# Retention and token-mixing MLP in one kernel: nine of the loads of k issued by ScalarE on its own DMA queue

## The chip, the cores and the metric

The kernel runs on one core of one Trainium2 chip. The metric is the device time of one execution in microseconds; below the time is better. One execution was profiled, and three others were timed without a profile.

The core has five engines that follow their own instruction lists in order: TensorE (PE, with its weight loads shown apart as PEld), VectorE (DVE), ScalarE (ACT), GpSimd (POOL) and SyncE (SP). A transfer is issued by an instruction in the list of one of them and then carried out by the core's 16 DMA engines. In the views, ACTq and SPq stand for ScalarE and SyncE while they issue a transfer.

## What is computed

The reference, cut to what matters (B 4, H 8, S 768, D 64, model width 512):

```python
gamma = 1.0 - 2.0 ** (-5.0 - np.arange(H))
for t in range(S):
    state = gamma * state + einsum('bhd,bhe->bhde', k[:, :, t], v[:, :, t])
    y[:, :, t] = einsum('bhd,bhde->bhe', q[:, :, t], state) / sqrt(D)
x = y.transpose(0, 2, 1, 3).reshape(B, S, H * D)

wq, wk = x @ w_q, x @ w_k
W_tok = einsum('bsd,btd->bst', wq, wk) / sqrt(64)
mixed = einsum('bst,btd->bsd', W_tok, x)
out = maximum(mixed, 0.0) @ w_out
```

A recurrence over the tokens gives x; a mixing of all tokens of a batch, a ReLU and a projection follow. All inputs and the output are float32: q, k and v are 6.29 MB each, the weights 1.31 MB and the output 6.29 MB.

## The kernel before

**The work.** The tokens are cut into 12 pairs of chunks, of 256 tokens each, three pairs to a batch. A pair is the unit of all that follows. Its k and q are loaded as float32, cast to bfloat16 and transposed; its v is loaded and scaled by a power of the decay. TensorE then forms the scores, the state and the rows of x, and in a later stage the mixing and the projection. Small steps do this, and each is one function:

- `ck`, `cq`: cast of k and of q (lines 623, 641, 660, through the helper `copy`, lines 138 to 141); `cv`: scaling of v on GpSimd (line 650). In pairs 2 to 11 `ck` and `cv` come in two parts, 0 and 1, each of two instructions on 64 partitions.
- `trk`, `trq`: transposes on TensorE (lines 667 and 700); `ek`, `eq`: their copies out of PSUM to `kq` (lines 689 and 725).
- `sc`, `eat`: scores and their masked copy (lines 740 and 757); `st`, `es`: state and its copy (lines 799 and 823); `in`, `ia`: the two parts of y (lines 779 and 828); `ex`: y to x (line 845).
- `xt`, `exT`, `wk`, `wq`, `ew`: x transposed and its products with the two small weights; `zm`, `ez`: their product with x per batch and its copy to `z_sb` (lines 948 and 966).
- `mx`, `r`, `pj`, `eo`: mixing, ReLU, projection and the copy of half an output to `o_st` (lines 976, 992, 1001 and 1013).

**The order of the work.** It is written out by hand. `ORDER` (line 16) is a list of tokens such as `cq.5:A`: step `cq` of pair 5 on ScalarE (A; V is VectorE, P is GpSimd); `@b` gives a PSUM bank. The loop at line 1050 emits them one by one, so each engine's list is the list of its tokens in this order. No scheduler changes it.

**The loads.** `LOADS` (line 55) is a second list: `k5` is the load of k of pair 5, `w`, `o0` and `o1` are weights, `s1` the store of output 1. `more_loads` (line 243) emits the loads in this order on SyncE, as far as the staging slots go (`SLOTS` is 7; a slot holds one input of three pairs and comes free when all three were cast). It is called when a slot comes free (`release`, line 261) and after each `eo`. So SyncE's list holds all loads in the order of `LOADS` and then the stores; the only transfer on another engine is half of the first k (line 240, ScalarE). A load of k or v of a pair is one transfer of 512 KB in rows of 512 bytes; a load of q is two transfers of 256 KB in rows of 1 KB (lines 170 to 176; in pairs 0 and 1 it is one transfer). Line 171 is the issue of q, line 188 that of k and v, line 223 that of `o0` and `o1`, line 1035 that of the stores.

**Completion semaphores.** In the built program all transfers, whichever engine issues them, take eight completion semaphores in turn. Before a transfer is issued, its issuing engine waits until the transfer eight places earlier, which had the same semaphore, has landed. So no more than eight transfers are under way.

Of the kernel before, what the change touches and what calls it, by code (L numbers as in the profile page):

```python
# [13 lines left out]


ORDER = """
ck.0.0:V ck.0.1:V fill.13@6 cv.0.1:P cq.0.0:A trk.0@0 fill.2@6 cq.0.1:V trq.0@0 ekq.0.1:V fill.2@6 fill.2@6
cv.0.0:P fill.2@6 fill.2@6 ekq.0.0:V sc.0.1@2 eat.0.1:V sc.0.0@0 st.0.0 fill.2@6 fill.2@6 ck.1:A trk.1@4
cq.1:A ck.2.1:A es.0.0:V in.0@2 eat.0.0:V ck.2.0:A ic.0@2 trq.1@4 ekq.1.1:V ekq.1.0:V cv.1:P ia.0.1@2
ia.0.0@2 st.0.1 es.0.1:V ex.0:V cv.3.0:P fill.2@6 cv.3.1:P sc.1.1@0 cq.2:A sc.1.0@4 st.1.0 cv.2.0:P  # L20
eat.1.1:V es.1.0:A eat.1.0:V ck.3.0:A xt.0:f@2 trk.2@0 ek.2:V fill.2@6 exT.0:V ia.1.1@4 cv.2.1:P ia.1.0@4
trq.2:f@0 eq.2:V ck.3.1:A ck.4.1:P ic.1@4 in.1@4 ex.1:V cv.4.0:P st.1.1 es.1.1:A sc.2.1@0 eat.2.1:V trk.3@2
cq.3:A ek.3:A sc.2.0@4 eat.2.0:V fill.2@6 fill.2@6 xt.1@0 cv.4.1:P st.2.0 es.2.0:A trq.3@0 eq.3:V fill.2@6
exT.1:V ck.4.0:A st.3.0 ck.5.0:P W:A es.3.0:A sc.3.0@4 eat.3.0:V in.2.0@2 in.2.1@2 ia.2.1@2 sc.3.1@0 wk.0@6
trk.4@4 ek.4:A eat.3.1:V ia.2.0@2 ex.2:V cq.4:A st.3.1 es.3.1:A wq.0@6 ew.0:A cv.5.0:P ia.3.0@0 in.3.1@0
ia.3.1@0 xt.2:f@2 trq.4:f@2 ck.5.1:A wq.1@6 cv.5.1:P wk.1@6 ew.1:A ex.3:V eq.4:V sc.4.0@0 xt.3@4 exT.2:V
sc.4.1@2 cq.6:P cq.5:A eat.4.0:V eat.4.1:V st.4.0 es.4.0:A wq.2@6 wk.2@6 ew.2:A trk.5:f@0 ek.5:A trq.5@4
eq.5:V zm.0.0@6 st.4.1 es.4.1:A ck.6.0:P zm.0.1@6 cv.6.0:P zm.0.2@6 ez.0.0:A ez.0.2:A sc.5.0@0 exT.3:V
eat.5.0:V in.4.1@2 ia.4.0@2 ez.0.1:A sc.5.1@4 ia.4.1@2 mx.2@0 in.4.0@2 eat.5.1:V wq.3@6 WO.1:A r.2:A st.5.0
wk.3@6 es.5.0:A ia.5.1@4 WO.0:A ia.5.0@4 cv.6.1:P mx.1@0 r.1:A in.5.0@4 ex.4:V in.5.1@4 ew.3:V trq.6@2  # L30
xt.4:f@2 pj.2.1@6 ck.6.1:A ex.5:V xt.5:f@4 eq.6:V pj.1.0@1 eo.1.0:A exT.4:V trk.6@2 pj.1.1@0 eo.2.1:V
exT.5:V wk.5@1 ck.7.1:A ek.6:V sc.6.0@2 sc.6.1@4 wq.5@1 wq.4@6 eo.1.1:V eat.6.0:V eat.6.1:V ck.7.0:A
cv.7.0:P st.6.0 wk.4@6 ew.5:A pj.2.0@0 mx.0@2 eo.2.0:V ck.8.1:P ew.4:A zm.1.2@6 es.6.0:A st.6.1 zm.1.0@6
zm.1.1@6 trk.7@4 in.6.1@0 ia.6.1@0 es.6.1:V cq.7:A r.0:A ez.1.0:V ia.6.0@0 pj.0.0@2 ez.1.2:V cq.8:P st.7.0
ck.8.0:A ek.7:V trk.8@3 trq.7@3 ez.1.1:A mx.3@5 ex.6:V xt.6@0 cv.7.1:P eq.7:V trq.8@0 es.7.0:A eo.0.0:A
r.3:A exT.6:V pj.0.1@2 ek.8:A eo.0.1:A eq.8:V sc.7.1@5 mx.5@0 r.5:A sc.8.0@3 st.7.1 es.7.1:A cv.8.0:P
eat.7.1:V eat.8.0:V pj.3.0@2 eo.3.0:A sc.7.0@0 eat.7.0:V cq.10:A cq.9:A sc.8.1@5 ia.7.1@3 cv.8.1:P eat.8.1:V
pj.3.1@2 eo.3.1:V st.8.0 in.7.1@3 in.7.0@3 ia.7.0@3 pj.5.0@0 trq.9:f@5 ex.7:V ia.8.1@1 ia.8.0@1 es.8.0:A
in.8.1@1 ck.9.0:A in.8.0@1 trq.10@3 eo.5.0:A ck.9.1:P eq.9:V trk.9@3 ex.8:V ck.10.1:P ck.10.0:A xt.7@5
pj.5.1@0 exT.7:A ek.9:V cv.9.0:P eq.10:V wk.6@1 eo.5.1:A mx.4@5 wq.6@1 ew.6:V wq.7@2 r.4:A xt.8@3 wk.7@2  # L40
trk.10@0 exT.8:V ek.10:V ck.11.1:A sc.9.1@5 eat.9.1:V pj.4.0@3 ew.7:A wk.8@0 sc.9.0@1 ck.11.0:A cq.11:P
eat.9.0:V cv.9.1:P wq.8@0 st.9.0 ew.8:A zm.2.1@4 es.9.0:A eo.4.0:A sc.10.0@5 eat.10.0:V zm.2.0@4 zm.2.2@4
ez.2.0:A ez.2.1:A st.9.1 ia.9.1@0 ia.9.0@0 cv.10.0:P in.9.1@0 trk.11@2 trq.11@2 ez.2.2:A mx.6@4 r.6:A ex.9:V
eq.11:V pj.4.1@6 es.9.1:V cv.10.1:P eo.4.1:A sc.10.1@0 eat.10.1:V ek.11:A pj.6.1@4 eo.6.1:A st.10.0 mx.8@5
r.8:A es.10.0:V xt.9@2 cv.11.0:P exT.9:V sc.11.0@0 eat.11.0:V st.10.1 es.10.1:A pj.6.0@4 sc.11.1@5
eat.11.1:V in.10.1@2 in.10.0@2 st.11.0 wq.9@0 es.11.0:A ia.10.1@2 ia.10.0@2 pj.8.0@1 eo.8.0:A cv.11.1:P
ia.11.0@5 ia.11.1@5 in.11.1@5 in.11.0@5 ex.10:V xt.10@2 exT.10:A pj.8.1@1 wk.9@0 ex.11:V eo.8.1:A xt.11@5
exT.11:V mx.7@2 r.7:V wk.10@1 ew.9:A wq.10@1 wk.11@0 ew.10:A wq.11@0 zm.3.1@1 ew.11:A zm.3.0@1 zm.3.2@1
eo.6.0:A pj.7.1@0 ez.3.1:A ez.3.2:A ez.3.0:A mx.9@1 r.9:A eo.7.1:V mx.10@3 mx.11@5 pj.7.0@0 pj.9.1@2
pj.9.0@1 r.11:A pj.11.1@5 pj.11.0@6 r.10:A pj.10.0@3 eo.11.1:A eo.7.0:V eo.10.0:A pj.10.1@0 eo.9.1:V  # L50
eo.9.0:V eo.11.0:V eo.10.1:A
# [22 lines left out]
def kernel(  # L74
# [89 lines left out]
    def load_pair(name, p, half=None, eng=None):  # L164
        st = pairs[p]
        if name == "q" and TYPES[p] != "2":
            st["q_st"] = slot("q" + str(p // NP)).rearrange("p (cp a j d) -> p cp a j d", cp=NP, a=4, j=4)[
                :, p % NP
            ]
            for u in range(2):  # L170
                nc.sync.dma_start(  # L171
                    out=st["q_st"].rearrange("(g u) a j d -> u g a (j d)", u=2)[u],
                    in_=q[p // NP, 4 * u : 4 * u + 4, p % NP * 2 * C : (p % NP + 1) * 2 * C, :].rearrange(
                        "a (g j) d -> g a (j d)", j=4
                    ),
                )
# [9 lines left out]
        cuts = [0, *PARTS.get(name + str(p), ()), C]
        for lo, hi in zip(cuts, cuts[1:]):
            (eng or nc.sync).dma_start(out=dst[lo:hi], in_=src[lo:hi])  # L188

    def load_batch(name, b):  # L190
        st = slot(name + str(b))
        if name == "q" or TYPES[b * NP] != "1":
            view = st.rearrange("p (h cp j d) -> p h cp j d", h=H, cp=NP, j=2)
            nc.sync.dma_start(
                out=view.rearrange("p h cp j d -> p h cp (j d)"),
                in_=SOURCES[name][b].rearrange("h (cp g j) d -> g h cp (j d)", cp=NP, j=2),
            )
            for cp in range(NP):
                pairs[b * NP + cp][name + "_st"] = view[:, :, cp]
        else:  # L200
            view = st.rearrange("p (h c d) -> p h c d", h=H, c=2 * NP)
            nc.sync.dma_start(
                out=view,
                in_=SOURCES[name][b].rearrange("h (c g) d -> g h c d", c=2 * NP),
            )
            for cp in range(NP):
                pairs[b * NP + cp][name + "_st"] = view[:, :, 2 * cp : 2 * cp + 2]
# [61 lines left out]


# [821 lines left out]
```

## Time and profile before

| | us |
|---|---|
| timed runs, each | 96.06, 98.69, 98.74 |
| their median | 98.69 |
| profiled execution, its own time | 95.44 |
| span of its instructions | 93.7 |

What the profiled execution adds to its span, 1.7 us, lies before and after the instructions. Busy time in four stretches, in us:

| stretch | PE | DVE | ACT | POOL | DMA, GB/s |
|---|---|---|---|---|---|
| 11 to 31 | 16.42 | 18.35 | 14.31 | 15.57 | 325 |
| 31 to 50 | 18.52 | 18.36 | 17.82 | 14.56 | 331 |
| 50 to 70 | 19.31 | 18.65 | 19.01 | 18.68 | 330 |
| 70 to 93.7 | 19.12 | 13.14 | 13.72 | 5.22 | 189 |

The first three stretches are 20, 19 and 20 us long: several engines and the transfers are full at the same time. The last load is issued at 59.89 us and lands at 66.9 us.

Waits are read as follows. In a timeline, a row in brackets such as `[3.01 <-DMA q_st<-in_q_dram]` says that the engine had been idle for 3.01 us before the row, until that transfer landed. Rows of the same kind that follow each other closely are merged, and idle times of a few hundredths are not shown.

### The profile page before, as it was taken

What the parts mean: (1) busy time and instruction counts of PE and PEld (TensorE: products, weight loads), DVE (VectorE), ACT (ScalarE), POOL (GpSimd) and SP (SyncE); (2) the same over time, 40 slices, a digit from 0 to 9 for tenths busy, and PEclk for the clock granted to TensorE, in tenths of its full rate; (3) what the DMA queues carried; (4) which work ended last, traced back from release to release, by engine and by line L of the source; (5) the groups of instructions that cost most, each with busy time, mean ns of one, the idle gap of its engine ahead of it and who ended that gap; (6) DMA issues with size and microseconds to landing.
All of it is one profiled execution on the core that took longest, in us unless ns stands there. A gap on an engine that the chain in (4) does not pass through costs nothing.

```text
span 93.7 us, 4105 instructions
## 1 busy us (share of the span) xinstructions
PE 83.0 (89%) x1775; PEld 54.6 (58%) x1793; DVE 74.1 (79%) x117; ACT 68.5 (73%) x116; POOL 60.9 (65%) x78
## 2 busy tenths in 40 slices
...
ACT  4320783399974999997989999999979438775540
POOL 6955207999999759889928999999999920000000
...
DMA  0999999999999999999999989999998400561982
GB/s 23 273 347 346 347 346 362 345 284 318 293 305 335 361 379 355 324 286 284 291 357 342 274 261 335 358 317 297 403 399 340 160 7 0 224 231 75 402 325 96
DMA packets 37970, 26.74 MB, mean 285 GB/s; under 512 B 2112, under 2 KB 34880, under 8 KB 37952
## 3 DMA queue, kind: packets, MB, share of 16 engines
...
HBM read 20.19 MB, written 6.29 MB: 282 GB/s over the span
## 4 chain that ended last, share of the span: by engine, by line
PE 38%; SPq 35%; DMA 15%; issue 3%; ACT 3%; DVE 1%
SPq L188 22%; PE banks L1004 16%; SPq L171 12%; DMA k_st<-in_k_dram 8%; DMA v_st<-in_v_dram 7%; PE banks L835 3%; PE banks L982 3%; PE banks L748 3%; PE banks L919 2%; PE banks L904 2%; PE banks L875 2%; PE banks L814 2%; PE banks L785 2%; PE banks L957 1%; PE banks L682 1%
## 5 line engine op out<-in xcount | busy, mean ns | idle before, releaser
L652 POOL TENSOR_TENSOR vs<-v_st,fv 64x512 bf16<-64x512 f32 x40 | 41.7, 1043 | 4.6 <-DMA v_st<-in_v_dram 2.2
L760 DVE TENSOR_TENSOR at_sb<-banks,cmaskr 128x1024 bf16<-128x1024 f32 x20 | 23.5, 1215 | 0.1
L1004 PE MATMUL banks<-wout_sb,relu 128*128 128x512 bf16 x83 | 22.4, 380 | 0.9 <-issue 0.3
L140 ACT CAST ks<-k_st 64x512 bf16<-64x512 f32 (+1 forms) x29 | 18.3, 632 | 3.7 <-DMA k_st<-in_k_dram 3.2
L141 DVE COPY kq<-banks 128x1024 bf16<-128x1024 bf16 x19 | 12.7, 684 | 4.2 <-PE banks L464 1.5
L140 ACT CAST qs<-q_st 128x1024 bf16<-128x1024 f32 (+1 forms) x9 | 8.9, 998 | 7.0 <-DMA q_st<-in_q_dram 7.0
L997 ACT ACTIVATE relu<-banks 128x1024 bf16<-128x1024 f32 x11 | 11.3, 1026 | 2.3 <-PE banks L1004 1.2
L414 PE MATMUL banks<-warm 128*128 128x512 bf16 x32 | 11.2, 483 | 1.9 <-DVE warm L273 1.3
L1004 PEld LDWEIGHTS <-relu 128*128 128x128 bf16 x96 | 8.1, 98 | 8.0 <-issue 0.2
L849 DVE TENSOR_TENSOR x_nat<-banks,fy 128x1024 bf16<-128x1024 f32 x10 | 12.1, 1216 | 0.8 <-PE banks L785 0.8
L140 ACT COPY o_st<-banks 128x512 f32<-128x512 f32 x15 | 8.9, 593 | 3.2 <-PE banks L1004 3.1
L141 DVE COPY o_st<-banks 128x512 f32<-128x512 f32 x9 | 6.2, 686 | 4.7 <-PE banks L1004 3.4
L141 POOL CAST ks<-k_st 64x512 bf16<-64x512 f32 x12 | 7.3, 609 | 2.7 <-DMA k_st<-in_k_dram 2.1
L442 POOL TENSOR_TENSOR vs<-v_st,fv 128x512 bf16<-128x512 f32 (+1 forms) x3 | 3.9, 1328 | 5.9 <-DMA v_st<-in_v_dram 5.9
L141 DVE COPY xT<-banks 128x1024 bf16<-128x1024 bf16 x10 | 6.8, 683 | 1.0 <-PE banks L875 0.8
L748 PE MATMUL banks<-kq 64*128 64x128 bf16 x160 | 7.6, 217 | 0.0
L835 PE MATMUL banks<-vs,at_sb 128*128 128x64 bf16 x160 | 7.1, 194 | 0.0
L414 PEld LDWEIGHTS <-warm 128*128 128x128 bf16 x37 | 3.6, 114 | 5.9 <-issue 3.0
L140 ACT CAST s_sb<-banks 128x256 bf16<-128x256 f32 x15 | 5.6, 373 | 1.2 <-PE banks L814 1.2
L748 PEld LDWEIGHTS <-kq 64*128 64x128 bf16 x160 | 4.9, 94 | 2.5 <-issue 1.5
L835 PEld LDWEIGHTS <-at_sb 128*128 128x128 bf16 x160 | 5.7, 98 | 1.0
L140 ACT COPY kq<-banks 128x1024 bf16<-128x1024 bf16 x5 | 5.1, 1017 | 0.7 <-PE banks L682 0.7
...
## 6 DMA issues: line engine op xcount, KB each, us to landing
v_st<-in_v_dram SPq DMA_DIRECT2D x12, 512.0 KB, 7.0
k_st<-in_k_dram SPq DMA_DIRECT2D x11, 512.0 KB, 6.1
...
out_dram<-o_st SPq DMA_DIRECT2D x9, 512.0 KB, 5.9
...
q_st<-in_q_dram SPq DMA_DIRECT2D x2, 512.0 KB, 5.5
...
```

Of the source, the lines that this page charges most:

```text
L140: return nc.scalar.copy(out=out, in_=in_)
L141: return ENGINES[e].tensor_copy(out=out, in_=in_)
L171: nc.sync.dma_start(out=st["q_st"].rearrange("(g u) a j d -> u g a (j d)", u=2)[u], in_=q[p // NP, 4 * u : 4 * u + 4, p % NP * 2 * C : (p ...
L188: (eng or nc.sync).dma_start(out=dst[lo:hi], in_=src[lo:hi])
L414: nc.tensor.matmul(out=bank32(b), lhsT=warm[:, 0:128], rhs=warm, start=True, stop=True)
L652: ENGINES[e].tensor_tensor(out=tokens_st(p, "v")[rows(j), c].rearrange("p hp x d -> p (hp x) d"), in0=pair_st(p, "v")[rows(c), :, j], in1= ...
L748: nc.tensor.matmul(out=ps[:, x, hi, c, :], lhsT=st["kT"][rows(x), hp, c, :], rhs=st["qT"][rows(x), hp, c, :], start=(hi == 0 and c == 0), ...
L760: ENGINES[e].tensor_tensor(out=st["at", half].rearrange("p x hi c t -> p (x hi c) t"), in0=st["at_ps", half].rearrange("p (n t) -> p n t", ...
L835: nc.tensor.matmul(out=y[:, x, c, hp, :], lhsT=st["at", half][:, x, hi, c, :], rhs=st["vs"][:, c, hp, x, :], start=first1(p, x), stop=Fals ...
L849: nc.vector.tensor_tensor(out=st["x"].rearrange("p c a i n -> p (c a i n)").rearrange("p (m x d) -> p x m d", x=2, d=D), in0=st["y_ps"].re ...
L997: nc.scalar.activation(out=dst, in_=st["mx_ps"], func=ACT.Relu)
L1004: nc.tensor.matmul(out=bank32(b), lhsT=st["relu"][:, a, j, :], rhs=wout_sb[:, a, :], start=(a == 0), stop=(a == NDM - 1),)
```

## The change

Loads of k of pairs 3 to 11 move from SyncE to ScalarE. In `LOADS` they are marked with a star; `load_token` passes the engine on. `more_loads` no longer emits as many loads as the slots allow: it may emit as many as it has been given (`due`), five at the start and then the number in each new token `ld.n` of `ORDER`. So each load of k stands in ScalarE's list where its `ld` stands among ScalarE's tokens. The loads and stores that stay on SyncE keep their order, and all computing instructions of all engines stand in the same order as before. A function for whole-batch loads that was not called is dropped.

```diff
-q0 v0 k1 q1 k2 v1 v3 q2 k3 v2 q3 k4 w v4 q4 k5 q5 v5 o1 q6 o0 k6 v6 k7 v7 q7 k8 q8 q10 v8 k9 q9 k10 v9 q11
-k11 v10 v11 s1 s2 s0 s3 s5 s4 s8 s6 s7 s9/1 s9/0 s11/1 s11/0 s10/0 s10/1
+q0 v0 k1 q1 k2 v1 v3 q2 k3* v2 q3 k4* w v4 q4 k5* q5 v5 o1 q6 o0 k6* v6 k7* v7 q7 k8* q8 q10 v8 k9* q9 k10*
+v9 q11 k11* v10 v11 s1 s2 s0 s3 s5 s4 s8 s6 s7 s9/1 s9/0 s11/1 s11/0 s10/0 s10/1
...
+EARLY = 5
...
-                nc.sync.dma_start(
+                (eng or nc.sync).dma_start(
...
-    def load_token(token):
+    def load_token(token, eng=None):
...
-            load_pair(token[0], int(token[1:]))
+            load_pair(token[0], int(token[1:]), eng=eng)
...
+    due = [0]
...
-            key = slot_of(token)
+            if not due[0]:
+                return
+            key = slot_of(token.rstrip("*"))
...
-            load_token(queue.pop(0))
+            due[0] -= 1
+            load_token(queue.pop(0).rstrip("*"), nc.scalar if token[-1] == "*" else None)
...
+    due[0] = EARLY
     more_loads()
...
-        if name == "fill":
+        if name == "ld":
+            due[0] += args[0]
+            more_loads()
+        elif name == "fill":
```

In `ORDER`, for instance, the line around pair 9 reads after the change:

```
sc.7.0@0 eat.7.0:V cq.10:A ld.2 cq.9:A sc.8.1@5 ia.7.1@3 cv.8.1:P eat.8.1:V pj.3.1@2 eo.3.1:V st.8.0
```

In the built program the nine loads stand in ScalarE's list as follows. The third column is the transfer eight places earlier in the program, for whose landing ScalarE waits there ("first" and "second" are the two transfers of a q or a weight).

| load | between which of ScalarE's tokens | waits for the landing of |
|---|---|---|
| k3 | `cq.1` and `ck.2.1` | half of k0 |
| k4 | `ck.2.0` and `cq.2` | q1 |
| k5 | `ck.3.0` and `ck.3.1` | v2 |
| k6 | `ew.0` and `ck.5.1` | q5, second |
| k7 | `ew.1` and `cq.5` | o1, second |
| k8 | `es.4.1` and `ez.0.0` | o0, second |
| k9 | `ew.5` and `ew.4` | q8, first (and a slot) |
| k10 | `ez.1.1` and `es.7.0` | v8 |
| k11 | `cq.10` and `cq.9` | q11, first |

SyncE's list after the change holds the other loads and the stores. Some of them now wait for a load of k that ScalarE issues: the second transfer of q8 for k6, v8 for k7, v9 for k8, and three stores for k9, k10 and k11.

More of the change, by code (lines that the diff above doesn't have):

```diff
@@ L16 @@
 ORDER = """
[L17 to L26, printed above, removed]
@@ L47 @@
[L47 to L51, printed above, removed]
+ck.0.0:V ck.0.1:V fill.13@6 ld.2 cv.0.1:P cq.0.0:A ld.1 trk.0@0 fill.2@6 cq.0.1:V trq.0@0 ekq.0.1:V fill.2@6
@@ new lines @@
+fill.2@6 cv.0.0:P fill.2@6 fill.2@6 ekq.0.0:V sc.0.1@2 eat.0.1:V sc.0.0@0 st.0.0 fill.2@6 fill.2@6 ck.1:A
+trk.1@4 cq.1:A ld.2 ck.2.1:A es.0.0:V in.0@2 eat.0.0:V ld.1 ck.2.0:A ic.0@2 trq.1@4 ekq.1.1:V ekq.1.0:V
+cv.1:P ia.0.1@2 ia.0.0@2 st.0.1 es.0.1:V ex.0:V cv.3.0:P fill.2@6 ld.3 cv.3.1:P sc.1.1@0 cq.2:A sc.1.0@4
+st.1.0 ld.1 cv.2.0:P eat.1.1:V es.1.0:A eat.1.0:V ck.3.0:A xt.0:f@2 trk.2@0 ek.2:V fill.2@6 exT.0:V ia.1.1@4
+ld.2 cv.2.1:P ia.1.0@4 trq.2:f@0 eq.2:V ck.3.1:A ld.1 ck.4.1:P ic.1@4 in.1@4 ex.1:V ld.1 cv.4.0:P st.1.1
@@ new lines @@
+es.1.1:A sc.2.1@0 eat.2.1:V trk.3@2 cq.3:A ek.3:A sc.2.0@4 eat.2.0:V fill.2@6 fill.2@6 xt.1@0 ld.2 cv.4.1:P
+st.2.0 es.2.0:A trq.3@0 eq.3:V fill.2@6 exT.1:V ck.4.0:A st.3.0 ck.5.0:P W:A es.3.0:A sc.3.0@4 eat.3.0:V
+in.2.0@2 in.2.1@2 ia.2.1@2 sc.3.1@0 wk.0@6 trk.4@4 ek.4:A eat.3.1:V ia.2.0@2 ex.2:V cq.4:A st.3.1 es.3.1:A
+wq.0@6 ew.0:A ld.2 cv.5.0:P ia.3.0@0 in.3.1@0 ia.3.1@0 xt.2:f@2 trq.4:f@2 ck.5.1:A wq.1@6 cv.5.1:P wk.1@6
+ew.1:A ex.3:V eq.4:V sc.4.0@0 xt.3@4 exT.2:V sc.4.1@2 ld.3 cq.6:P cq.5:A eat.4.0:V eat.4.1:V st.4.0 es.4.0:A
@@ new lines @@
+wq.2@6 wk.2@6 ew.2:A trk.5:f@0 ek.5:A trq.5@4 eq.5:V zm.0.0@6 st.4.1 es.4.1:A ck.6.0:P zm.0.1@6 ld.2
+cv.6.0:P zm.0.2@6 ez.0.0:A ez.0.2:A sc.5.0@0 exT.3:V eat.5.0:V in.4.1@2 ia.4.0@2 ez.0.1:A sc.5.1@4 ia.4.1@2
+mx.2@0 in.4.0@2 eat.5.1:V wq.3@6 WO.1:A r.2:A st.5.0 wk.3@6 es.5.0:A ia.5.1@4 WO.0:A ia.5.0@4 ld.1 cv.6.1:P
+mx.1@0 r.1:A in.5.0@4 ex.4:V in.5.1@4 ew.3:V trq.6@2 xt.4:f@2 pj.2.1@6 ck.6.1:A ex.5:V xt.5:f@4 eq.6:V
+pj.1.0@1 eo.1.0:A exT.4:V trk.6@2 pj.1.1@0 eo.2.1:V exT.5:V wk.5@1 ck.7.1:A ek.6:V sc.6.0@2 ld.1 sc.6.1@4
@@ new lines @@
+wq.5@1 wq.4@6 eo.1.1:V eat.6.0:V eat.6.1:V ck.7.0:A cv.7.0:P st.6.0 wk.4@6 ew.5:A pj.2.0@0 mx.0@2 eo.2.0:V
+ld.2 ck.8.1:P ew.4:A zm.1.2@6 es.6.0:A st.6.1 zm.1.0@6 zm.1.1@6 trk.7@4 in.6.1@0 ia.6.1@0 es.6.1:V cq.7:A
+r.0:A ez.1.0:V ia.6.0@0 pj.0.0@2 ez.1.2:V cq.8:P st.7.0 ck.8.0:A ek.7:V trk.8@3 trq.7@3 ez.1.1:A mx.3@5
+ex.6:V xt.6@0 ld.2 cv.7.1:P eq.7:V trq.8@0 es.7.0:A eo.0.0:A r.3:A exT.6:V pj.0.1@2 ek.8:A ld.1 eo.0.1:A
+eq.8:V sc.7.1@5 mx.5@0 r.5:A sc.8.0@3 st.7.1 es.7.1:A cv.8.0:P eat.7.1:V eat.8.0:V pj.3.0@2 eo.3.0:A
@@ new lines @@
+sc.7.0@0 eat.7.0:V cq.10:A ld.2 cq.9:A sc.8.1@5 ia.7.1@3 cv.8.1:P eat.8.1:V pj.3.1@2 eo.3.1:V st.8.0
+in.7.1@3 in.7.0@3 ia.7.0@3 pj.5.0@0 ld.1 trq.9:f@5 ex.7:V ia.8.1@1 ia.8.0@1 es.8.0:A in.8.1@1 ck.9.0:A
+in.8.0@1 trq.10@3 eo.5.0:A ck.9.1:P eq.9:V trk.9@3 ex.8:V ck.10.1:P ck.10.0:A xt.7@5 pj.5.1@0 exT.7:A ek.9:V
+cv.9.0:P eq.10:V wk.6@1 eo.5.1:A mx.4@5 wq.6@1 ew.6:V wq.7@2 r.4:A xt.8@3 wk.7@2 trk.10@0 exT.8:V ek.10:V
+ck.11.1:A sc.9.1@5 eat.9.1:V pj.4.0@3 ew.7:A wk.8@0 sc.9.0@1 ck.11.0:A cq.11:P eat.9.0:V cv.9.1:P wq.8@0
@@ new lines @@
+st.9.0 ew.8:A zm.2.1@4 es.9.0:A eo.4.0:A sc.10.0@5 eat.10.0:V zm.2.0@4 zm.2.2@4 ez.2.0:A ez.2.1:A st.9.1
+ia.9.1@0 ia.9.0@0 cv.10.0:P in.9.1@0 trk.11@2 trq.11@2 ez.2.2:A mx.6@4 r.6:A ex.9:V eq.11:V pj.4.1@6
+es.9.1:V cv.10.1:P eo.4.1:A sc.10.1@0 eat.10.1:V ek.11:A pj.6.1@4 eo.6.1:A st.10.0 mx.8@5 r.8:A es.10.0:V
+xt.9@2 cv.11.0:P exT.9:V sc.11.0@0 eat.11.0:V st.10.1 es.10.1:A pj.6.0@4 sc.11.1@5 eat.11.1:V in.10.1@2
+in.10.0@2 st.11.0 wq.9@0 es.11.0:A ia.10.1@2 ia.10.0@2 pj.8.0@1 eo.8.0:A cv.11.1:P ia.11.0@5 ia.11.1@5
```

44 lines of the change are left out of this document (4 added, 40 removed).

## The prediction

> **What bounds the kernel now.** I read the page first: which engines are full, and when.
>
> ```profile
> span 93.7 us, 4105 instructions
> PE 83.0 (89%) x1775; PEld 54.6 (58%) x1793; DVE 74.1 (79%) x117; ACT 68.5 (73%) x116; POOL 60.9 (65%) x78
> ACT  4320783399974999997989999999979438775540
> POOL 6955207999999759889928999999999920000000
> DMA  0999999999999999999999989999998400561982
> k_st<-in_k_dram SPq DMA_DIRECT2D x11, 512.0 KB, 6.1
> ```
>
> A slice is 2.34 us. The DMA engines are full from 2.3 us to about 70 us, whatever the compute engines do, and ScalarE is full from about 30 to 73 us. A load of k lands 6.1 us after its issue, though 512 KB take about 1.5 us of the stream (20.2 MB in some 62 us is 1.6): several loads always lie ahead of it. Next the chain of waits in order of time:
>
> ```profile
> 26.76 6.98 DMA v_st<-in_v_dram
> ...
> 33.81 1.45 SPq L188
> ...
> 42.14 7.11 DMA k_st<-in_k_dram
> ...
> 49.30 0.62 issue
> 49.92 0.63 ACT ks L140
> ```
>
> v5 lands at 26.76 + 6.98 = 33.74, and SyncE issues v6 at 33.81: v6 is eight transfers after v5, and this is the wait for the semaphore of the eighth transfer back, seen at work. k8 (issued at 42.14) lands at 49.25, and from there the chain is compute. Third, ScalarE's timeline at the places where the change puts a load:
>
> ```profile
> 10.91 1.05 ACT L140 CAST qs<-q_st 128x1024 bf16<-128x1024 f32 x1 [0.45 <-DMA q_st<-in_q_dram]
> 12.40 2.52 ACT L140 CAST ks<-k_st 64x512 bf16<-64x512 f32 x4 [0.44 <-DMA k_st<-in_k_dram]
> 17.93 1.04 ACT L140 CAST qs<-q_st 128x1024 bf16<-128x1024 f32 x1 [3.01 <-DMA q_st<-in_q_dram]
> ...
> 29.64 1.04 ACT L140 CAST qs<-q_st 128x1024 bf16<-128x1024 f32 x1 [1.22 <-DMA q_st<-in_q_dram]
> ...
> 45.98 0.75 ACT L140 CAST wkq<-banks 128x256 bf16<-128x256 f32 x2
> ...
> 49.27 1.26 ACT L140 CAST ks<-k_st 64x512 bf16<-64x512 f32 x2 [0.33 <-DMA k_st<-in_k_dram]
> 50.56 0.37 ACT L140 CAST z_sb<-banks 64x256 bf16<-64x256 f32 x1
> ...
> 55.98 1.99 ACT L140 CAST qs<-q_st 128x1024 bf16<-128x1024 f32 x2
> ```
>
> From 29.64 us (q4 landed) to 73.7 us ScalarE waits for nothing but 0.56 us for a matmul at 42.97 and 0.33 for k8. Whatever is put into its list there has no idle time to go into. Before 29.64 it idles for q and k, so there a delay can be covered. Last, single loads, each from the view of the transfers of one tile in a narrow window; this is the first half of q11:
>
> ```profile
> L171 SPq DMA_DIRECT2D q_st<-in_q_dram x1: 2090/2090/2090, 54.4 to 54.4; - x1
> ...
> DMA to landing us min/median/max: 6.7/6.7/6.7
> ```
>
> Issue plus latency is its landing: 54.42 + 6.7 = 61.1. In the same way: v2 13.65 + 7.2 = 20.9; q5's second half 26.11 + 6.1 = 32.2; o1's second 30.10 + 5.0 = 35.1; o0's second 32.72 + 5.1 = 37.8; q8's first 42.79 + 7.1 = 49.9; v8 46.34 + 7.1 = 53.5. These are the landings ScalarE is to wait for.
>
> **What the change removes.** SyncE loses nine issues, 0.40 to 2.39 us each, 8.1 us in all. That is worth nothing: SyncE is held back by the transfers, whose stream has no gap. The same bytes in another order end when they ended. A load of k issued by ScalarE no longer lies behind SyncE's backlog: it lands between 3.7 us (the half of k0 from SyncE at the start) and 6.1 us after issue, and what it overtakes, q and v, lands later by up to its 1.5 us. The wait for k8 goes: 0.33 us on ScalarE, 1.88 on GpSimd at 49.40. GpSimd's share is covered, since PE and ScalarE are full there.
>
> **What it adds to ScalarE.** An issue of k costs 0.40 (shortest row on SyncE) to 2.39 us (longest, the backlog full); I take the median row, 0.60, since ScalarE's own queue is nearly empty; its one issue of 256 KB took 0.47. It could be less than 0.40 if it ran beneath the instruction ahead; no row shows that. With it comes the wait for the eighth transfer back, and all of ScalarE's later steps are queued behind both. Place by place, with the lag that ScalarE has then:
>
> k3, at 11.96: `ck.2.1` waits until 12.40 for k2 anyway, so 0.2. k4, at 14.9: covered by the 3.01 us of waiting for q2; that cover holds, as q2 itself comes later: k3 and k4 overtake it, 0 to 3.0 us, say 2.5, so 20.3. Against that k3, for which `ck.3.0` waited until 19.37, is long there: `ck.3.0` starts at about 21.7, lag 2.3. k5 at 20.65 + 2.3: v2 (20.9) has landed; 0.6 for the issue, lag 2.9. Then the idle 0.69 (a matmul) and 1.22 (q4) take up 1.2 to 1.9 of it; but k5 now overtakes q4, which lands when k5 did, 30.9 instead of 29.55. `cq.4` starts 1.4 us late.
>
> From here nothing is covered. k6, at 31.34 + 1.4 = 32.7: q5 (32.2) is there; 0.6, lag 2.0. k7, at 33.10 + 2.0 = 35.1: o1 landed at 35.1 and now has a part of k6 ahead, so 35.1 to 36.6, say 35.6: wait 0.5 and 0.6, lag 3.1. k8, at 35.92 + 3.1 = 39.0: o0 at 37.8, with k6 and part of k7 ahead 37.8 to 40.8, say 40.0: wait 1.0 and 0.6, lag 4.7. k9, at 46.3 + 4.7 = 51.0: q8 (49.9) is there; 0.6, lag 5.3; less the 0.33 for k8, 5.0. k10, at 50.93 + 5.0: v8 (53.5) is there; 0.6, lag 5.6. k11, between the two casts of the row at 55.98, at 57.0 + 5.6 = 62.6: q11 (61.1) is there; 0.6, lag 6.2.
>
> The end result does not hang on the small waits. Even with all other terms at nothing, ScalarE can't pass k9 before 49.9 (lag 3.6 + 0.6), nor k11 before 61.1 (4.1 + 0.6 = 4.7), with `cq.9` and all after it behind. Only a faster stream of transfers could lower this.
>
> **Who waits for ScalarE.** `cq.9` ended at 57.97 and its transposes started at 58.94, so 0.97 of slack; `ez.2` ended at 69.01 and `mx.6` started on PE at 69.06: slack 0.05. So PE gets 6.1 of the 6.2. From 69 us PE works to 89.8 almost without a stop, and nothing there shortens. SyncE's new waits (v8 for k7 and so on) cost nothing: each of those k is issued over 5 us ahead. GpSimd has v6 later by up to 3 us but no longer waits 1.88 for k8, lag about 1, under ScalarE's.
>
> **The sum.** 95.44 (profiled; span 93.7 and 1.7 around it) + 1.4 + six issues 3.6 + waits 1.5 - 0.33 - 0.05 = 101.5. The median of the runs shown is 98.69, 3.25 above the profiled execution, with the lowest at 96.06: the same sum from there is 104.8. I cannot tell which sort of run will be the median, and forecast the middle, 103.2.
>
> [...]
>
> **Rivals.** *Faster*: two queues fill the DMA engines better. From 42.8 to 66.9 us 14 units of 512 KB took 1.72 us each, early ones 1.5. At 1.5 throughout, q8 would land at about 48.1 and k8 in time. If moreover an issue costs ScalarE next to nothing, PE gains at most GpSimd's 1.88: 93.6. Against it: the DMA share is over 1.0 in these stretches, so there is no idle to fill. It decides if q8 lands before 46.3. *Small loss*: that faster stream, but issues at 0.4: the floor at k11 becomes 58.6 - 57.0 + 0.4 = 2.0, with the earlier lag of about 3: 98.4 profiled, 99 to 101 in the runs. *No change*: PE, not ScalarE, is the bound from 50 us, and the lag vanishes in slack; 95 to 97. Against it: slack of 0.05 to 0.97 where I looked. [...] That k isn't moved can be excluded: the built program shows nine issues in ScalarE's list.
>
> **Chances.** Lag as summed 0.60; one queue at a time 0.13; small loss 0.14, of which 0.12 is over 2%; no change 0.06; faster 0.07. 2% is about what a measurement of this kernel can tell from no change. So slower 0.85, same 0.08, faster 0.07. Range 99.0 to 107.0: from the lowest run, 96.06, with the smaller lag of 2.9, to the upper runs, 98.7, with 6.1 and half of the lock's 4.3. It leaves out faster, no change, and the upper part of the lock, under 0.2.
>
> **What would show it.** Right: nine ACTq rows of about 0.6 us; ScalarE's `cq.4` at about 31, `cq.9` near 63; rows behind k7, k8, k9 or k11 that start just after o1, o0, q8 or q11 land; the last load still landing at 66 to 68; no wait for k8. [...] The forecast falls if ScalarE passes k9 before 48 us.

## The result and the profile after

The changed kernel took 101.07 us in the median of four runs (100.01 to 102.30), the kernel before 97.38 beside it (96.06 to 98.74): the ratio is 1.044, 95% interval 1.030 to 1.058. A second set on another chip gave 101.14 against 96.22, 1.053 (1.046 to 1.060). It is slower, by 4 to 5 us. The forecast was 103.2 (99.0 to 107.0).

Some executions of these kernels are disturbed and longer, the traced one of the first set among them; the ratios leave them out, and so differ a little from the quotients of the medians. The trace read here is that of the second set (100.59 us, span 98.8); "before" is the trace that the prediction read (span 93.7). The difference to be explained is 5.1 us.

First the page of the changed kernel: totals, the slices (now 2.47 us each) of ScalarE, GpSimd, the granted clock and the DMA engines, the code-loading queue, and the loads of k.

```profile
span 98.8 us, 4119 instructions
PE 86.6 (88%) x1793; PEld 55.3 (56%) x1793; DVE 74.5 (75%) x117; ACT 68.8 (70%) x116; POOL 60.8 (62%) x78
...
ACT  4321781095867999976999999959997917676640
POOL 6847126957999999999799960799999500000000
PEclk9999999965599999999999999999999999999999
DMA  0999999999999999999999999982300500550982
...
q8 instruction: 14, 0.23, 0.9%
...
k_st<-in_k_dram ACTq DMA_DIRECT2D x9, 512.0 KB, 8.6
```

ScalarE's busy time is what it was (68.8 against 68.5), but the page doesn't count issues as busy, so it tells nothing of their cost; a run below does. The clock, nowhere low before 90 us in the kernel before, is at 6, 5, 5 tenths in slices 9 to 11. And a load of k takes longer on its own queue, 8.6 us to landing against 6.1. Next the chain of waits, as start and length in us:

```profile
13.15 9.59 DMA v_st<-in_v_dram
22.74 0.02 issue
22.76 0.37 ACTq L189
23.14 0.04 issue
23.18 0.62 ACT ks L141
...
40.68 1.08 issue
...
47.71 0.26 issue
...
59.30 0.51 issue
...
65.00 0.73 issue
```

Two things are on it that were not on the chain before. v2 lands at 22.74, ScalarE issues k5 at 22.76, and the cast of k3 follows: the wait for the eighth transfer back, at k5. And from 40 to 85 us the chain is nearly all TensorE, with these four pieces called "issue" in it, 2.58 us in all: the engine stood still, and the profile shows no semaphore that it waited for. ScalarE's timeline at the places the prediction spoke of:

```profile
11.06 1.04 ACT L141 CAST qs<-q_st 128x1024 bf16<-128x1024 f32 x1 [0.44 <-DMA q_st<-in_q_dram]
11.07 0.37 ACTq L189 DMA_DIRECT2D k_st<-in_k_dram  x1
...
19.57 1.04 ACT L141 CAST qs<-q_st 128x1024 bf16<-128x1024 f32 x1 [4.47 <-DMA q_st<-in_q_dram]
...
23.18 1.26 ACT L141 CAST ks<-k_st 64x512 bf16<-64x512 f32 x2 [1.13 <-DMA v_st<-in_v_dram]
...
32.10 0.37 ACTq L189 DMA_DIRECT2D k_st<-in_k_dram  x1
32.19 1.05 ACT L141 CAST qs<-q_st 128x1024 bf16<-128x1024 f32 x1
...
59.26 0.37 ACTq L189 DMA_DIRECT2D k_st<-in_k_dram  x1
59.66 1.99 ACT L141 CAST qs<-q_st 128x1024 bf16<-128x1024 f32 x2
```

`cq.2` starts at 19.57 (17.93 before), `cq.4` at 32.19 (29.64). The issue of k3 (11.07, row ACTq) runs while the cast of q1 (11.06 to 12.10), which stands ahead of it, is at work; k6 is issued at 32.10, ahead of `cq.4`, though `cq.4`, `es.3.1` and `ew.0` stand ahead of it in the list. So ScalarE's list was not worked off strictly in order here: a transfer was issued while computing instructions ahead of it still ran or were queued.

The lag of ScalarE's steps against before: `cq.2` 1.64 us, second part of `ck.3` 2.53, `cq.4` 2.55, `z_sb` 2.77 (38.62 against 35.85), `ck.8.0` 3.57, `exT.7` 5.10 (66.27 against 61.17), end 5.1. Half comes before 32 us and stays; the other half comes after 40 us and is as large as the four "issue" pieces: 2.55 + 2.58 = 5.13. This is an account of two traces; the runs below test its parts.

**The first half: TensorE idles and its clock falls.** TensorE's timeline at 20.67, and a table by stretch of the same trace (busy time of PE, PEld, DVE, ACT, POOL with instruction counts, granted clock, DMA share, GB/s):

```profile
20.67 0.61 PE L693 MATMUL banks<-identity_q,qs 128*128 128x128 bf16 x4 [1.85 <-ACT qs L141]
```

```profile
18.00:19.00 1.00, 0.64 (x32) 0.54 (x32) 1.00 (x3) 0.00 (x0) 0.96 (x1) 1.00 1.13 351
...
21.00:27.00 6.00, 5.30 (x83) 3.18 (x81) 4.30 (x4) 4.59 (x7) 4.29 (x5) 0.50 1.09 322
27.50:31.00 3.50, 3.41 (x108) 2.57 (x104) 2.64 (x4) 2.50 (x6) 3.23 (x5) 1.00 1.11 368
```

q2 comes late, TensorE idles 1.85 us, and then the granted clock is 0.50 from about 20.7 to 27.5 us: 83 matmuls in 6 us, and afterwards 108 in 3.5. Before, TensorE's longest idle time between 14 and 31 us was 0.89 and the clock stayed at 1.00 there (the row with that idle time, and the clock's slices):

```profile
30.74 0.62 PE L708 MATMUL banks<-identity_q,qs 128*128 128x128 bf16 x8 [0.89 <-ACT qs L140]
...
PEclk9999999999999999999999999999999999999997
```

Here 1.85 us without a matmul stand ahead of a low stretch of 6.8 us; in the first set's trace of the changed kernel 2.29 us stand ahead of one of 6.83, from 21.4 us. In five other traces of this case a low stretch of 3.4 us stands between 16 and 29 us. What sets these lengths is not shown.

**The second half: TensorE waits for code.** TensorE's timeline at the first of the four pieces, and ahead of it the DMA queues between 39.44 and 40.38 us (packets, MB, share):

```profile
q10 hardware_dynamic: 425, 0.22, 76.6%
q1 hardware_dynamic: 180, 0.09, 31.2%
q8 instruction: 1, 0.02, 6.2%
```

```profile
40.48 0.21 PE L770 MATMUL banks<-s_sb,kq 64*128 64x64 bf16 x2
41.77 0.26 PE L770 MATMUL banks<-s_sb,kq 64*128 64x64 bf16 x6 [1.08 <-issue]
```

Queue 8 loads instructions, 14 blocks of 16 KB (0.23 MB) in the span; one runs here, 39.44 to 40.38. Counted in the trace, each of the four stops stands within two of TensorE's weight load number 226 + 128 n, and those are 256 instructions apart (128 weight loads and as many matmuls; the page has 1793 of each). The next block was fetched after TensorE had entered one, and not at once: here TensorE entered the block at 35.36, the fetch began 4.08 later, and TensorE went on 1.39 after its end. Before, the same fetch began 1.85 after the entry, and TensorE did not stop.

### The profile page after: what moved, and what is told of

It is laid out like the page before. It is cut to its first block, busy times and chain, and to the rows that moved or that the text cites. A ratio compares the mean times of both kernels' runs of the same rounds, so it can differ in the third digit from the quotient of the medians.

```text
span 100.6 us, 4119 instructions
## 1 busy us (share of the span) xinstructions
PE 85.1 (85%) x1793; PEld 54.9 (55%) x1793; DVE 74.7 (74%) x117; ACT 68.9 (68%) x116; POOL 61.0 (61%) x78
## 3 DMA queue, kind: packets, MB, share of 16 engines
q10 hardware_dynamic: 9888, 4.98, 16.6%
## 4 chain that ended last, share of the span: by engine, by line
PE 58%; SPq 12%; DMA 10%; DVE 7%; issue 6%; ACT 3%; ACTq 0%; DVEq 0%
PE banks L989 20%; SPq L189 10%; DMA v_st<-in_v_dram 10%; PE banks L733 4%; PE banks L820 4%; PE banks L967 4%; PE banks L904 3%; PE banks L799 3%; PE banks L667 3%; PE banks L889 3%; PE banks L860 3%; DVE at_sb L745 2%; PE banks L942 2%; PE banks L770 2%; DVE kq L142 2%
## 5 line engine op out<-in xcount | busy, mean ns | idle before, releaser
L989 PE MATMUL banks<-wout_sb,relu 128*128 128x512 bf16 x96 | 23.9, 380 | 0.3 <-issue 0.3
L399 PE MATMUL banks<-warm 128*128 128x512 bf16 x37 | 11.7, 457 | 1.3 <-DVE warm L258 1.3
L733 PE MATMUL banks<-kq 64*128 64x128 bf16 x160 | 8.3, 226 | 1.1 <-issue 1.0
L667 PE MATMUL banks<-identity,ks 64*128 64x64 bf16 x144 | 4.5, 196 | 1.7 <-ACT ks L141 0.8
```

The costliest lines, as they stand in the source:

```text
L399: nc.tensor.matmul(out=bank32(b), lhsT=warm[:, 0:128], rhs=warm, start=True, stop=True)
L667: nc.tensor.transpose(ps[:, j, hp, c], st["ks"][rows(j), c, hp].rearrange("p x d -> p (x d)"), identity[rows(j), rows(j)],)
L733: nc.tensor.matmul(out=ps[:, x, hi, c, :], lhsT=st["kT"][rows(x), hp, c, :], rhs=st["qT"][rows(x), hp, c, :], start=(hi == 0 and c == 0), ...
L989: nc.tensor.matmul(out=bank32(b), lhsT=st["relu"][:, a, j, :], rhs=wout_sb[:, a, :], start=(a == 0), stop=(a == NDM - 1),)
```

## The experiments

Times are medians; the ratio to the kernel before, run on the same chip, stands behind with its 95% interval. Medians of before there were 96.22, 96.20, 96.40 and 95.68. A line with a star is a load on ScalarE.

**The two kernels once more.** The changed one:

> The changed kernel once more, for a second trace. The first trace of it shows a lag of 2.8 us at the cast of q4, and then five idle gaps of PE of 0.3 to 1.4 us in the middle of runs of equal matmuls, before instructions that wait for no semaphore, each right after a fetch of PE's instructions: 4.2 us after 30 us in all. Theory F (fetches of PE's instructions come late when a second queue moves data): such gaps again, over 1.5 us in sum after 30 us, and the time is 94 plus 2.8 plus their sum. Theory S (the prediction: ScalarE's lag comes from the issues and the waits for the eighth transfer back): the gaps are an accident of one execution and are gone, and the time stays at 100 to 101.

101.14 us, 1.053 (1.046 to 1.060): its trace is the one above. And the kernel before, as a test of the measure:

> The kernel before once more, for a second trace beside its first, in which each fetch of PE's instructions (16 KB, one for each 128 weight loads) began 1.3 to 3.2 us after PE had entered the block before, and only one block, the first, was late. Theory F: one queue of data gives delays in that band again, up to 3.3, and no or one late block after 30 us; the two traces of the changed kernel have 3.7 to 4.8 between 36 and 62 us. If delays of 4 us turn up here too, the second queue isn't what makes them.

96.62 us, 1.009 (1.003 to 1.015), span 94.7: the same kernel differs by 0.9%, so nothing below one per cent is read as a difference.

**Only the issues.** The kernel before, all loads on SyncE, and ScalarE issues nine loads of 8 KB (into an unused tile) at the nine places:

```diff
+        if name == "tiny":
+            i = tiny[0]
+            tiny[0] += 1
+            nc.scalar.dma_start(out=pad[:, 16 * i : 16 * i + 16], in_=q[0, 0, 0:128, 0:16])
```

> The kernel before with all its loads on SyncE, and nine loads more on ScalarE at the places that the change gives to k3 to k11, each of 8 KB (128 rows of 64 bytes) into a tile that nobody reads. It has the issues without the moved data. Theory S: 0.4 to 0.6 us for each of the six places after 30 us, 2.4 to 3.6 us over the kernel before. Theory O: the issues run beside the instructions ahead of them and cost 0 to 0.5 us in all; a second queue that carries almost nothing does not bring the gaps of theory F either.

96.61 us, 1.008 (1.004 to 1.012): no more than the kernel before against itself. Nine issues on ScalarE cost nothing that can be measured. (They carry almost no data, so this is the price of issuing alone.) ScalarE's timeline shows one beneath a cast that started first:

```profile
29.27 1.04 ACT L138 CAST qs<-q_st 128x1024 bf16<-128x1024 f32 x1 [0.71 <-DMA q_st<-in_q_dram]
29.42 0.34 ACTq L1056 DMA_DIRECT2D pad<-in_q_dram  x1
```

**Only k3 to k5 on ScalarE.**

```diff
-v5 o1 q6 o0 k6* v6 k7* v7 q7 k8* q8 q10 v8 k9* q9 k10*
-v9 q11 k11* v10 v11
+v5 o1 q6 o0 k6 v6 k7 v7 q7 k8 q8 q10 v8 k9 q9 k10
+v9 q11 k11 v10 v11
```

> Only k3, k4 and k5 on ScalarE; k6 to k11 back on SyncE in the old order. Theory O (k3, k4 and k5 overtake q2, v2 and q4, PE runs dry and its clock drops): cq.4 2.5 to 3 us late, granted clock 0.96, 2.5 to 3.5 us over the kernel before. Theory S: 1.4 us over it. Theory F: few gaps after 30 us, as only one queue moves data there.

98.42 us, 1.025 (1.018 to 1.031). `cq.2` 19.59, `cq.4` 32.42, clock 0.83 between 11 and 31 us: the whole first half of the loss is in it. The interval lies clear of the full change's, run on the same chip: the six later loads cost about 2.7 us more.

**Only k6 to k11 on ScalarE.**

```diff
-v1 v3 q2 k3* v2 q3 k4* w v4 q4 k5* q5
+v1 v3 q2 k3 v2 q3 k4 w v4 q4 k5 q5
```

> Only k6 to k11 on ScalarE; k3 to k5 back on SyncE. Theory S: six issues and the waits at k9 and k11, 4.2 to 4.8 us over the kernel before. Theory O: no lag at cq.4, granted clock 0.99, and as an issue runs beside ScalarE's work, 0 to 1 us over the kernel before, or less than it, if the waits of GpSimd and ScalarE for k8 go. Theory F: gaps of PE without a semaphore after 30 us, 1 to 4 us in sum, which are the whole loss.

101.21 us (98.42 to 101.73). Three of the four runs are 5.0 to 5.5 us over the kernel before and one is 2.2 over it, so the price of this part is not settled by these runs. ScalarE's timeline in the traced one, the longest (101.73), shows at the place of k8:

```profile
35.70 0.40 ACT L141 CAST s_sb<-banks 128x256 bf16<-128x256 f32 x1
39.35 0.38 ACTq L189 DMA_DIRECT2D k_st<-in_k_dram  x1
39.76 1.16 ACT L141 CAST z_sb<-banks 128x256 bf16<-128x256 f32 x3 [3.66 <-DMA q_st<-in_q_dram]
```

In this kernel the transfer eight before k8 is the first half of q6, which landed at 39.33; ScalarE stood 3.66 us until it could issue. Without the early lag it comes to k8 too soon. TensorE idles 2.76 us behind it, and the granted clock is then 0.50 for 6.8 us from 40.4.

**The same with k8 later.** k8's issue moved from ahead of `ez.0` to ahead of the cast of k7:

```diff
-wq.2@6 wk.2@6 ew.2:A trk.5:f@0 ek.5:A trq.5@4 eq.5:V zm.0.0@6 st.4.1 es.4.1:A ck.6.0:P zm.0.1@6 ld.2
+wq.2@6 wk.2@6 ew.2:A trk.5:f@0 ek.5:A trq.5@4 eq.5:V zm.0.0@6 st.4.1 es.4.1:A ck.6.0:P zm.0.1@6
...
-exT.5:V wk.5@1 ck.7.1:A ek.6:V sc.6.0@2 ld.1
+exT.5:V wk.5@1 ld.3 ck.7.1:A ek.6:V sc.6.0@2 ld.1
```

(`ld.1` ahead of `cv.6.1` is dropped too.)

> As e_late (k6 to k11 on ScalarE), but k8 stands in ScalarE's list just ahead of the cast of k7's second part, 8 us later. In e_late ScalarE stood still for 3.66 us at k8's old place until q6 landed, the transfer eight places back, and PE for 2.75. Theory W (this wait is nearly the whole loss of e_late): no idle time of ScalarE for a transfer that it doesn't cast, and the time 2.5 to 3.7 us under e_late's, so 96 to 98. Against it: k8 now lands after 50 and the wait for it takes back 1 to 2 us; or blocks of PE come late (theory F) and take 1 to 3.

101.1 us, 1.057 (1.048 to 1.066): the wait of 3.66 is gone and the time is not better. In its place, in the trace: a late block of code, 1.12 us up to 39.87; ScalarE idle 0.67 for k8 at 52.10; and at 62.05 this:

```profile
61.56 0.37 ACTq L189 DMA_DIRECT2D k_st<-in_k_dram  x1
62.05 1.04 ACT L141 CAST qs<-q_st 128x1024 bf16<-128x1024 f32 x1 [2.20 <-POOL ks L142]
```

k11 is issued 0.02 us after the first half of q11, the transfer eight places ahead, landed (61.54), and the cast of q9 follows: that fits a wait of ScalarE at k11, which the prediction had as a floor, better than the GpSimd that the profile puts it down to. So the theory that the wait at k8 was nearly the whole price fell, but a wait of the same kind came elsewhere. The late loads cost 4.9 us in this form and the early ones 2.2, and both together 4.9 (by the medians): the parts do not add up.

**k8 earlier, all on SyncE.** In the kernel before, k8 ahead of q7:

```diff
-k7 v7 q7 k8 q8
+k7 v7 k8 q7 q8
```

> The kernel before with one load moved in SyncE's list: k8 ahead of q7 instead of behind it. No load on ScalarE. It removes the wait for k8 (0.33 us on ScalarE, 1.88 on GpSimd at 49 us). If that wait was on the path: 0.3 to 1.9 us under the kernel before. If PE and ScalarE were full anyway, as the prediction holds: within 0.4 us of it.

97.15 us, 1.017 (1.012 to 1.023). No gain: the waits of 0.33 and 1.88 us for k8 are gone, and ScalarE waits 1.55 us for q7 instead, which k8 has overtaken (its cast starts at 49.14). Here the earlier load of k made the load of q late. This trace also has the clock at 0.50 for 3.4 us from 21.9, in a stretch where the kernel is the one before, and `cq.4` is only 0.45 late (30.09).

**The order of landing without a second queue.** The kernel before, all on SyncE, but with k3 listed ahead of q2 and k4 ahead of v2, close to the order in which the changed kernel issues them:

```diff
-q0 v0 k1 q1 k2 v1 v3 q2 k3 v2 q3 k4 w
+q0 v0 k1 q1 k2 v1 v3 k3 q2 k4 v2 q3 w
```

> The kernel before, all loads on SyncE, but with k3 listed ahead of q2 and k4 ahead of v2: the order in which the changed kernel's transfers land, without a second queue and without any issue on ScalarE. Theory O (the early loss is the order of landing: q2 and v2 come 1.5 to 2 us later, TensorE idles, and its clock falls): cq.2 near 19.5, ck.3.1 near 23, clock of 11 to 31 us near 0.83, time as with k3 to k5 on ScalarE, 97.8 to 98.9. Rival Q (the second queue or ScalarE's issuing does it, whatever the order): cq.2 near 18, time 96.2 to 97.0.

98.62 us, 1.028 (1.005 to 1.050), `cq.2` 19.56, `cq.4` 32.00. The page has the same dip of the clock:

```profile
span 96.7 us, 4105 instructions
...
PEclk9999999995559999999999999999999999999999
```

and the table by stretch (first line 11 to 31 us):

```profile
11.00:31.00 20.00, 15.10 (x398) 10.22 (x400) 14.69 (x18) 11.88 (x20) 13.32 (x13) 0.83 1.04 313
31.00:50.00 19.00, 17.53 (x421) 13.69 (x420) 18.11 (x22) 17.30 (x31) 16.46 (x19) 1.00 1.04 323
```

So the early loss needs neither ScalarE's issue nor its queue: k3 and k4 ahead of q2 and v2 are enough. The interval of the time is wide, and by it alone this would not be shown; the steps and the clock in the trace are those of the run with k3 to k5.

**TensorE kept busy.** The changed kernel with six matmuls on a constant tile, whose result is not used, ahead of the transposes of q2:

```diff
-ld.2 cv.2.1:P ia.1.0@4 trq.2:f@0 eq.2:V ck.3.1:A
+ld.2 cv.2.1:P ia.1.0@4 fill.6@6 trq.2:f@0 eq.2:V ck.3.1:A
```

> The changed kernel with six fill matmuls more, on data that nobody reads, ahead of the transposes of q of pair 2, where PE waits 1.9 to 2.3 us for q2. Theory O2 (the wait makes PE's clock drop to about half from 20 to 28 us, and that makes up half of the lag at cq.4): granted clock 0.99, cq.4 1 to 2 us earlier, and the time 1 to 2 us under the changed kernel's. If the lag comes from the late landings of q2 and v2 alone: clock up, time within 0.3 us of the changed kernel's.

99.79 us, 1.036 (1.027 to 1.046): by the medians 1.3 us better than the changed kernel, which ran on another chip; the intervals touch. In the trace (an execution of 100.38) the dip of the clock did not go: it is half as long, 3.4 us from 25.4, and `cq.4` starts at 32.11, no earlier than in the changed kernel (32.19). So how much of the early 2.55 us is the clock, and how much the late landings, stays open.

**And k5 behind the cast of k3.**

```diff
-ld.2 cv.2.1:P ia.1.0@4 fill.6@6 trq.2:f@0 eq.2:V ck.3.1:A ld.1 ck.4.1:P
+cv.2.1:P ia.1.0@4 fill.6@6 trq.2:f@0 eq.2:V ck.3.1:A ld.3 ck.4.1:P
```

> The changed kernel with six idle-time matmuls ahead of the transposes of q2, as in the run with them alone (99.8), and moreover k5's issue moved behind the second part of the cast of k3, so that this cast no longer waits for v2. Theory O2 (the 1.1 us that ScalarE stands there for v2 is on the path): wait under 0.3, cq.4 about 0.5 to 1 us earlier, time 98.7 to 99.3. Rival (TensorE and the clock are the limit there, not that wait): 99.5 to 100.2.

99.29 us, 1.041 (1.030 to 1.051). The wait for v2 is gone, the clock between 20 and 28 us is 1.00 (it is 0.50 for 3.4 us before, from 16.6), and `cq.4` starts at 30.00: all but 0.36 of the early lag is repaired. Against the run before, the time can't be told apart. ScalarE's timeline shows what takes its place:

```profile
33.87 0.37 ACTq L189 DMA_DIRECT2D k_st<-in_k_dram  x1
34.28 1.04 ACT L141 CAST qs<-q_st 128x1024 bf16<-128x1024 f32 x1 [0.83 <-DMA w_st<-in_moe_w_out_dram]
...
37.91 0.37 ACTq L189 DMA_DIRECT2D k_st<-in_k_dram  x1
38.33 1.15 ACT L141 CAST z_sb<-banks 128x256 bf16<-128x256 f32 x3 [1.23 <-PE banks L733]
```

k7 is issued 0.02 us after o1 landed (33.85), k8 0.02 after o0 (37.89). These are the two waits that the prediction put at 0.5 and 1.0 us: 0.83 and 1.23. (The profile names TensorE for the second; the products that `z_sb` needs had ended at 36.97, and the landing in the trace fits the issue.) In the changed kernel the lag hid them: it reached the two places at 34.89 and 38.20, with o1 and o0 landed at 33.65 and 36.77.

**And k7 and k8 back on SyncE.**

```diff
-k6* v6 k7* v7 q7 k8* q8
+k6* v6 k7 v7 q7 k8 q8
```

> The kernel of the run before (changed kernel, six idle-time matmuls, k5's issue behind the cast of k3: 99.29), and moreover k7 and k8 back on SyncE in the same places of the list of loads. There ScalarE stood 0.83 us until o1 landed, eight transfers ahead of k7, and 1.23 us at the place of k8, issued 0.02 us after o0 landed. Theory W2 (with the early lag gone these two waits are the next loss): both idle times vanish, z_sb starts 1 to 2 us earlier than 38.33, time 97.2 to 98.2. Rival F (late instruction blocks and the lag behind them are what counts, and they stay): time 98.8 to 99.6.

98.89 us, 1.036 (1.029 to 1.042). Both waits are gone and `z_sb` starts at 36.32, 2.0 us earlier, as the first theory said. The median is that of its rival, the traced execution, 97.74, lies in the range of the first, and the ratio can't be told from the run before: the time does not decide. The next rows of the trace show why little was won:

```profile
36.32 1.15 ACT L141 CAST z_sb<-banks 128x256 bf16<-128x256 f32 x3
37.38 1.04 ACT L141 CAST wout_sb<-w_st 128x1024 bf16<-128x1024 f32 x1
39.43 1.02 ACT L982 ACTIVATE relu<-banks 128x1024 bf16<-128x1024 f32 x1 [1.01 <-PE banks L967]
```

TensorE stood 0.80 us for a block there, fetched from 36.90 to 37.87, and went on at 39.11; in the run before it passed the same place at 39.53, with the fetch ended at 38.12. Of the 2.0 us 0.4 are left there: who arrives earlier waits for the code.

**k9 to k11 back on SyncE**, k3 to k8 on ScalarE:

```diff
-q8 q10 v8 k9* q9 k10* v9 q11 k11* v10 v11
+q8 q10 v8 k9 q9 k10 v9 q11 k11 v10 v11
```

> The changed kernel with k9, k10 and k11 back on SyncE, in the same places of the list of loads; k3 to k8 stay on ScalarE. Theory F (what is lost after 50 us are late instruction blocks under the two-queue stream and k9 to k11 issued late by a lagging ScalarE): GpSimd's wait of 3.67 us for k10 shrinks to under 1, the late blocks near 59 and 65 us (0.51 and 0.73) shrink, time 99.6 to 100.5 against 101.1. Rival E (all was lost before 50 us, the rest only follows): GpSimd's wait shrinks too, but the time stays at 100.8 to 101.4. Should SyncE's list be blocked by the waits of k9 to k11 for slots, the time would rise above 101.4.

100.06 us, 1.047 (1.037 to 1.058): not to be told from the full change. In the changed kernel GpSimd had a new wait, since the lagging ScalarE issued k10 only at 53.48 and it landed at 62.18 (58.23 before):

```profile
62.30 1.28 POOL L142 CAST ks<-k_st 64x512 bf16<-64x512 f32 x2 [3.67 <-DMA k_st<-in_k_dram]
```

Here that wait is gone, and a block late by 1.58 us at 63.58 stands in the trace. So to take GpSimd's wait away was not enough.

The traces side by side, one execution each, in us. "Late blocks" are TensorE's stops at a block's end after 30 us that the profile puts down to no semaphore; "fetch delay" is the median time from entering a block to the start of the next fetch, over seven blocks from about 30 to 66 us.

| trace | `cq.2` | `cq.4` | clock, 11 to 31 | late blocks | fetch delay | span |
|---|---|---|---|---|---|---|
| before | 17.93 | 29.64 | 1.00 | 0 | 2.3 | 93.7 |
| landing order, SyncE alone | 19.56 | 32.00 | 0.83 | 0.86 | 2.9 | 96.7 |
| k3 to k5 on ScalarE | 19.59 | 32.42 | 0.83 | 0.62 | 3.2 | 96.8 |
| changed | 19.57 | 32.19 | 0.83 | 2.58 | 3.7 | 98.8 |
| k9 to k11 back | 19.45 | 32.07 | 0.83 | 2.03 | 3.0 | 98.6 |
| fill, k5 later | 19.58 | 30.00 | 0.91 | 0.74 | 3.8 | 97.6 |
| and k7, k8 back | 19.69 | 30.03 | 1.00 | 0.80 | 3.3 | 96.0 |

In the first five rows the span over before is the lag of `cq.4` and the late blocks together, within 0.5 us. The sixth has the waits of 0.83 and 1.23 beside them. In the last, both columns give 1.2 of the 2.3 us; the rest is not accounted for. A second trace of the kernel before had 0.77 us of late blocks, at 72 us, and a delay of 2.5 in the median, with two delays of 4.0 (at 59.9 and 66.2). So the kernel before is near that edge already, and by the text put down ahead of that run, delays of 4 us there mean that the second queue alone isn't what makes them.

None of these kernels beats the kernel before.

## Why the prediction was right or wrong

**The direction and the range** were right: slower by more than 2%, 101.07 inside 99.0 to 107.0. The sum, 101.5 on the scale of a profiled execution, stands against 100.59. But its terms were not the ones that made the time: what was counted and not paid (issues and waits, 5.1) and what was paid and not counted (1.15 more at `cq.4`, 2.58 of late blocks) cancelled but for about 1 us. That the number came out so near is luck. Of the signs, `cq.4` came at 32.19 (about 31 was named), the cast of q9 near 60.7 (63), the last load landed at 68.4 (66 to 68), and the wait of ScalarE for k8 was gone. Against it, the first half of q11 landed at 53.69, where the sum had 61.1. The range and the chances also hold a "lock", one queue at a time, at 4.3 us for the six issues: no run shows that term. What the runs showed in its place are rows of 0.37 to 0.44 us on ScalarE, in the midst of SyncE's.

**"I take the median row, 0.60": six issues, 3.6 us.** Measured: nothing. The rows are 0.37 to 0.44 us and lie beneath other work; nine issues alone gave 1.008 (1.004 to 1.012). The prediction had seen that it could run beneath the instruction ahead, and that no row showed it. This is the largest mis-sized term.

**"Waits 1.5": k7 for o1, k8 for o0.** Not paid in the changed kernel, since the early lag of 2.5 us brought ScalarE there after the landings. The mechanism is real: with the early lag repaired the same places cost 0.83 and 1.23, where 0.5 and 1.0 were written. In the kernel with k8 moved, k11 cost 2.20 behind q11. The same wait was paid at a place where the prediction had it covered: k5 waited for v2, "has landed", 1.13 us, because k4 had overtaken v2 as well (22.74 against 20.9).

**"`cq.4` starts 1.4 us late", q4 behind k5.** `cq.4` was 2.55 late, and not for q4, which landed no later (29.38; before, 29.55). What failed is the step "covered by the 3.01 us of waiting for q2". It covers ScalarE, whose lag at `cq.2` was the 1.64 of q2's delay. The prediction did not ask what TensorE does meanwhile: it idles, and runs the next 6.8 us at half clock. (How much of the lag is the clock's is open, as said above.) The cost of a late input was read from the engine that waits for it, and not from the one behind. (One reading of the trace of before was incomplete: between 29.64 and 73.7 us ScalarE also idles 0.54 us at 69.55. No term hangs on it.)

**"Even with all other terms at nothing", the floors at q8 (49.9) and q11 (61.1)** did not hold. They were SyncE's landings of before, taken as fixed. With nine loads out of its list SyncE issued the rest earlier: the first half of q11 at 48.56 instead of 54.42, as the view of the transfers of q in a narrow window says:

```profile
L172 SPq DMA_DIRECT2D q_st<-in_q_dram x1: 667/667/667, 48.6 to 48.6; - x1
...
DMA to landing us min/median/max: 5.1/5.1/5.1
```

48.56 + 5.1 = 53.7, and ScalarE came to k11 only at 59.26. This landing moved with the order of issue, and the sum held it still. The faster stream of the rivals was there too: 359 GB/s from 31 to 50 us, against 331 before. It brought no gain: behind the wait for v2 no piece of the chain is a wait for a load.

**A load of k lands "between 3.7 us" and "6.1 us after issue":** 8.6 in the median. The transfers of both queues were served side by side (76.6% and 31.2% of the 16 engines' time between 39.44 and 40.38), and the empty queue did not put k3 ahead: issued at 11.07, it landed at 19.66, and the second half of q2, issued by SyncE at 12.50, at 19.49.

**Nothing stood in the sum for code loading.** The late blocks are 2.58 of the 5.1 us. That they are on the path is shown by the chain of waits; that the six late loads cost 2.7 us is shown by the run without them, and in the traces the late blocks make 1.96 of that (2.58 against 0.62). Why the fetches come later is argued only: the delay is 1.6 to 2.5 us in the three traces where nothing was changed before k8, 3.0 to 3.8 in the four of the table in which loads of k after k5 go through ScalarE, but also 3.2 with k3 to k5 alone, and 2.9 with one queue in the other order and with the nine tiny loads. Single delays of 4.0 stand in a trace of the kernel before. Whether the second queue, the fuller stream or the lag itself delays them stays open; no run moved TensorE's code.

**The rivals.** *One queue at a time*, to which the chances give 0.13, fell: k7's row takes 0.37 us at 34.89, in the middle of SyncE's issues of q7 and q8, which the trace of SyncE shows without a pause:

```profile
34.34 5.48 SPq L172 DMA_DIRECT2D q_st<-in_q_dram  x4
```

The first of the four took 3.23 us, to 37.57, and ScalarE did not wait for its end. In the trace of before, too, ScalarE and SyncE both issued 256 KB at 0.80 us, side by side in 0.47 and 0.44. Of *faster* the stream came true (q8's first half landed at 46.10, just before the 46.3 that it named), and ScalarE's wait for k8 went (k8 landed at 48.08); there was no gain, as ScalarE was at that place 3.57 us later than before. *No change* fell with the lag of 5.1 at the end: no slack took it up. *Small loss*, 98.4 profiled, was nearest by its mechanism (cheap issues, faster stream, an early lag), and missed the clock and the blocks.
